# Attention in pairs of tiles, and both weight matrices converted in one pass, in a fused attention and feed-forward kernel

## The chip, the cores and the metric

The kernel runs on one core of a Trainium2 chip. TensorE (PE) multiplies, VectorE (DVE), ScalarE (ACT) and GpSimd (POOL) work on whole tiles, SyncE (SP) issues the transfers between memory and chip. The metric is the device time of one execution in microseconds, as the median of several runs.

## What is computed

For 8 batches, 8 heads, 576 positions and a head size of 64, each chunk of 64 positions attends to itself. The result, 4608 tokens of 512 values, goes through two matrices with a sigmoid gate between them:

```python
scores = scale * np.matmul(q_c, k_c.transpose(0, 1, 2, 4, 3))
scores = scores - np.max(scores, axis=-1, keepdims=True)
attn = np.exp(scores)
attn = attn / (np.sum(attn, axis=-1, keepdims=True) + 1e-09)
out = np.matmul(attn, v_c)
...
h = x @ w_in                              # 512 -> 2048
g = h * (1.0 / (1.0 + np.exp(-1.702 * h)))
return (g @ w_out).astype(np.float32)     # 2048 -> 512
```

The inputs arrive as float32, the two matrices as float64.

## The kernel before

**Tiles and blocks.** The tokens are 36 tiles of 128, in 9 blocks of 4 tiles (TB). The 2048 inner values are 16 columns (NF) of 128. One step g is one block and one column j: `h_pe` multiplies x by w_in's column into `hp`, `g_hi` and `g_lo` form the gated value, `o_pe` multiplies it by w_out's rows into the four accumulators po0 to po3, one a tile. There are 144 such steps.

**Three products for one.** x, g and both matrices are kept as a high and a low part, and each product is three matmuls over 512 columns: low by high, high by high, high by low (lines 474 to 476 for h, 509 to 511 for o; the first step works in two halves of 256 columns, lines 487 to 489).

**Weights.** The 8-byte words are turned into floats on the chip. `plan_w` does this for 32 parts, each 512 words wide, even parts for w_in and odd ones for w_out: a load, two ACT operations (`c0`, lines 173 and 174), three DVE operations (`c1`, 179, 180, 183), ACT's high part (188) and DVE's low part (191). All 32 stay on the chip and serve all 9 blocks, so conversion happens only beside the first block and a little beyond.

**Attention.** `plan_att` treats one tile of 128 tokens. Tiles 0 to 3 ("first") come before the feed-forward and keep their buffers in the slots of the last weights, four slots a tile; tiles 0 to 5 are transposed by PE (`t_pe`, line 272, `e_pe`, line 347), all others by DVE (`t_dve`, 294, `e_dve`, 367, eight transposes of 32x256). Then for each tile: scores (`s_pe`, line 317), maximum and subtraction (324, 325), the exponential on ACT (328), sum and reciprocal (332 to 335), normalisation on POOL (338), the product with v (`x_pe`, 379) and the high and low part of x (392, 395). Tiles from 4 on are worked on while the feed-forward of the block before runs. The profile lists each of the 16 float32 score matmuls of a tile, and each of the 16 with v, as two instructions, so a tile's block has 32.

**What sets the order.** Every step is handed to a `Plan` with an engine, a cost in microseconds, a rank and the buffers that it takes and gives. A greedy list scheduler runs through simulated time and lets each engine take the ready step of lowest rank; the order so found is the order in which each engine's instructions stand in the program, and nothing reorders them on the chip. SP issues all loads and stores from one queue.

Of the kernel before, what the change touches and what calls it, by code (L numbers as in the profile page):

```python
# [98 lines left out]
def tile_chunk_attention_ffn(  # L99
# [14 lines left out]
    P = 128  # L114
# [4 lines left out]
    NWP = 2 * NF  # L119
# [5 lines left out]
    NPE = 6  # L125
    NTMP = 6
    WARM = 7

# [10 lines left out]
    buffers = {b: 2 for b in ("hp", "att", "raw", "v", "tr", "e", "et", "x", "g", "ob")}  # L139
    buffers.update({f"w{p}": 1 for p in range(NWP)})  # L140
    buffers.update({f"po{t}": 1 for t in range(TB)})
    buffers.update(tmp=NTMP)
    plan = Plan(buffers)

    def att_rank(u):
        if u < TB:
            return u - 95
        return (-2, 5, 9, 10)[u - TB] if u < 2 * TB else NF * (u // TB - 1) + 4 * (u % TB) - 2
# [4 lines left out]
    def plan_w(p):  # L153
        j, part = divmod(p, 2)
        rank = 0.986 * j - (1.2 if part else 3.5)

        def words():
            word = lambda t, i: w_raw[p].bitcast(t).rearrange("p (n w) -> p n w", w=2)[:, :, i]
            return word(F32, 1), word(I32, 1), word(I32, 0), word(U32, 0)

        def load():
            w_raw[p] = raw = const.tile([P, 512], I64, tag=f"w{p}", name=f"raw_{p}")
            if part == 0:
                nc.sync.dma_start(
                    raw.rearrange("p (cc f) -> p cc f", cc=NCC),
                    w_in[:, j * P : (j + 1) * P].rearrange("(cc p) f -> p cc f", p=P),
                )
            else:
                nc.sync.dma_start(raw, w_out[j * P : (j + 1) * P, :])

        def c0():
            hf, hi, li, lu = words()
            nc.scalar.activation(hf, hf, AF.Copy, scale=2.0**-112)
            nc.scalar.activation(li, lu, AF.Copy, scale=2.0**-29)

        def c1():
            hf, hi, li, lu = words()
            w_tmp[p] = tmp = more.tile([P, 512], I32, tag="wtmp", name=f"wtmp_{p}")
# [29 lines left out]
    raw_t, v_t, t_t, e_t, s_t = {}, {}, {}, {}, {}  # L208
# [11 lines left out]
    def plan_att(u):  # L220
        first = u < TB
        pe = u < NPE
        k_act = u in (2, 5)
        rank = att_rank(u)
        slot = lambda i: f"w{NWP - 1 - (4 * u + i)}"
        res = lambda i, name: slot(i) if first else name

        def buf(i, tag, shape, name):

            pool, tag = (const, slot(i)) if first else (two, tag)  # L230
            return pool.tile(shape, F32, tag=tag, name=f"{name}_{u}")

        def load_rows():
            raw_t[u] = t = buf(0, "raw", [P, 2, H, D], "rows")
            for i, src in enumerate((q, k)):
                for b, s, o, c in spans(u * P, P):
                    nc.sync.dma_start(
                        t[o : o + c, i], src[b, :, s : s + c, :].rearrange("h s d -> s h d")
                    )

        def load_qk(i, n):

            if i == n == 0:
# [13 lines left out]

        def load_v():
            v_t[u] = t = buf(2, "v", [P, H, D], "v")
            for b, s, o, c in spans(u * P, P):  # L260
                nc.sync.dma_start(t[o : o + c], v[b, :, s : s + c, :].rearrange("h s d -> s h d"))

        def t_pe():
            raw = raw_t.pop(u)
            if first:
                ps = [ps_h.tile([P, NP, P], F32, tag="hp", name=f"qkTp_{u}_{i}") for i in range(2)]
            else:
                both = ps_a.tile([P, 2, NP, P], F32, tag="att", name=f"qkTp_{u}")
                ps = [both[:, 0], both[:, 1]]
            for i in range(2):  # L270
                for n in range(NP):
                    nc.tensor.transpose(  # L272
                        ps[i][:, n],
                        raw[:, i, 2 * n : 2 * n + 2, :].rearrange("p h d -> p (h d)"),
                        ident,
                    )
            s_t[u] = ps
            t_t[u] = buf(1, "tr", [P, 2, NP, P], "qkT")

        def t_q():  # L280
            nc.scalar.activation(t_t[u][:, 0], s_t[u][0], AF.Copy)

        def t_k():
            if k_act:
                nc.scalar.activation(t_t[u][:, 1], s_t[u][1], AF.Copy)
            else:
                nc.vector.tensor_copy(t_t[u][:, 1], s_t[u][1])

        def t_dve():
            raw = raw_t.pop(u)  # L290
            t_t[u] = t = buf(1, "tr", [P, 2, NP, P], "qkT")
            o = (u % 2) * 4
            for i in range(2):
                nc.vector.transpose(  # L294
                    t[:, i].rearrange("p n (t j) -> p n t j", j=32), raw[:, i, :, o : o + 4, :]
                )

        def s_pe():

            t = t_t.pop(u)  # L300
            e_t[u] = buf(3, "e", [P, NP, 2, CH], "e")
            if first:
                sc = ps_o.tile([P, NP, 2, CH], F32, tag=f"po{u % 2}", name=f"s_{u}")
                s_t[u] = sc
            elif pe:
                sc = ps_a.tile([P, NP, 2, CH], F32, tag="att", name=f"s_{u}")
                s_t[u] = sc
            else:
                sc = ps_a.tile([P, 2, 2, NP, CH], F32, tag="att", name=f"s_{u}")
                s_t[u] = sc[:, :, 0].rearrange("p h n j -> p n h j")  # L310
            for n in range(NP):
                for c in range(2):
                    for h in range(2):
                        r = slice(64 * h, 64 * h + 64)
                        cols = slice(64 * c, 64 * c + 64)
                        o = sc[r, n, c, :] if pe else sc[cols, h, 0, n, :]
# [12 lines left out]

        def s_sum():  # L330
            z = two.tile([P, NP, 2], F32, tag="z", name=f"z_{u}")
            nc.vector.tensor_reduce(z, e_t[u], axis=AX.X, op=ALU.add)
            nc.vector.tensor_scalar_add(z, z, 1e-9)
            s_t[u] = two.tile([P, NP, 2], F32, tag="r", name=f"r_{u}")
            nc.vector.reciprocal(s_t[u], z)  # L335

        def s_norm():
            nc.gpsimd.tensor_tensor(e_t[u], e_t[u], bc(s_t.pop(u)), op=ALU.mult)  # L338

        def e_pe():  # L340
# [267 lines left out]
```

## Time and profile before

| | before |
| --- | --- |
| median of 3 runs | 899.12 us (898.19 to 900.22) |
| profiled execution, own time | 901.2 us |
| its span | 899.4 us |
| PE busy | 875.3 us, 97% |
| DVE busy | 439.6 us, 49% |
| ACT busy | 366.4 us, 41% |
| POOL busy | 38.8 us, 4% |

A busy share is an average over the span. The first 30 us are loads and the attention of the first four tiles, until about 140 us weights are converted beside the feed-forward, and behind that the feed-forward of one block runs beside the attention of the next. What bounds a stretch is read from the row of that stretch, and from the waits of the engine that ends last in it. Times of an instruction on PE overlap with its neighbour's, so its cost is the distance from one start to the next.

### The profile page before, as it was taken

The page shows a single profiled execution, that of the slowest core. Times are in us where ns is not written, and L with a number is a line of the kernel's source. Part 1 is how long each engine was busy: PE and PEld are TensorE (multiplying, and loading weights), DVE is VectorE, ACT ScalarE, POOL GpSimd, SP SyncE. Part 2 cuts the span into 40 slices and gives each one's busy share as a digit, 9 for nine tenths or more (in the row PEclk, how much of TensorE's full clock was granted, in tenths as well). Part 3 has the DMA queues.
Part 4 walks back from the last instruction along what each step waited for, and adds up shares of the span by engine and source line. Part 5 has one row for each costly group of instructions (what it writes and reads, how often), then busy time and mean ns, then how long its engine had stood idle before and what let it go on. Part 6 is the DMA issues. An engine that isn't in the chain of part 4 may idle for free.

```text
span 899.4 us, 14557 instructions
## 1 busy us (share of the span) xinstructions
PE 875.3 (97%) x5858; PEld 705.1 (78%) x5858; DVE 439.6 (49%) x810; ACT 366.4 (41%) x554; POOL 38.8 (4%) x42
## 2 busy tenths in 40 slices
PE   7899969999999999999999999999999999999998
PEld 6688747888888888888888888888888888888886
DVE  5999996544444444444444444445444454311111
ACT  3998744333333333333433333334333333322222
POOL 1000000000000000000000000000000000000000
PEclk9799989999999999999999999999999999999999
DMA  9995232322322122212221312132210010001001
GB/s 239 319 321 140 43 57 64 63 50 51 70 66 38 29 39 63 42 31 48 64 44 26 57 59 42 31 55 65 42 30 12 24 48 1 1 1 47 1 0 48
DMA packets 199141, 55.51 MB, mean 62 GB/s; under 512 B 184225, under 2 KB 192417, under 8 KB 199073
## 3 DMA queue, kind: packets, MB, share of 16 engines
q1 hardware_dynamic: 199072, 54.57, 26.4%
q8 instruction: 46, 0.75, 0.4%
q14 instruction: 23, 0.18, 0.1%
HBM read 45.09 MB, written 9.44 MB: 61 GB/s over the span
## 4 chain that ended last, share of the span: by engine, by line
PE 95%; DVE 3%; ACT 1%; issue 0%; POOL 0%; POOLq 0%; ACTq 0%; DVEq 0%
PE po L509 15%; PE hp L474 15%; PE po L510 15%; PE hp L476 14%; PE po L511 14%; PE hp L475 14%; PE s L317 3%; PE x L379 2%; DVE eT L367 1%; PE qkTp L272 1%; DVE wtmp L180 0%; PE warm L563 0%; PE eTp L347 0%; DVE wtmp L183 0%; DVE w L191 0%
## 5 line engine op out<-in xcount | busy, mean ns | idle before, releaser
L500 DVE TENSOR_TENSOR g_l<-hp,g_h 128x512 fp32r<-128x512 f32 x144 | 99.4, 690 | 315.9 <-ACT g_h L496 314.9
L509 PE MATMUL po<-w,g_l 128*128 128x512 f32 x576 | 229.9, 399 | 0.7 <-ACT w L188 0.7
L476 PE MATMUL hp<-x_h,w 128*128 128x512 f32 x572 | 224.9, 393 | 5.7 <-DVE w L191 5.7
L474 PE MATMUL hp<-x_l,w 128*128 128x512 f32 x572 | 228.1, 399 | 1.9 <-ACT w L188 1.9
L510 PE MATMUL po<-w,g_h 128*128 128x512 f32 x576 | 227.2, 394 | 0.0
L511 PE MATMUL po<-w,g_h 128*128 128x512 f32 x576 | 225.1, 391 | 0.2 <-DVE w L191 0.2
L475 PE MATMUL hp<-x_h,w 128*128 128x512 f32 x572 | 224.4, 392 | 0.0
L495 ACT ACTIVATE hp<-hp 128x512 f32<-128x512 f32 x144 | 84.1, 584 | 172.2 <-PE hp L476 171.4
L496 ACT ACTIVATE g_h<-hp 128x512 fp32r<-128x512 f32 x144 | 86.1, 598 | 122.8 <-PE po L511 120.8
L476 PEld LDWEIGHTS hp<-x_h,w 128*128 128x128 f32 x572 | 107.8, 188 | 30.9 <-DVE w L191 7.2
L474 PEld LDWEIGHTS hp<-x_l,w 128*128 128x128 f32 x572 | 107.9, 189 | 26.9 <-ACT w L188 2.3
L509 PEld LDWEIGHTS po<-w,g_l 128*128 128x128 f32 x576 | 108.3, 188 | 26.3 <-ACT w L188 1.1
L511 PEld LDWEIGHTS po<-w,g_h 128*128 128x128 f32 x576 | 108.4, 188 | 24.5 <-DVE w L191 0.6
L475 PEld LDWEIGHTS hp<-x_h,w 128*128 128x128 f32 x572 | 108.0, 189 | 22.3
L510 PEld LDWEIGHTS po<-w,g_h 128*128 128x128 f32 x576 | 108.6, 189 | 21.2
L367 DVE STREAM_TRANSPOSE eT<-e 32x256 f32<-32x256 f32 x240 | 104.6, 436 | 36.0 <-POOL e L338 32.6
L392 ACT ACTIVATE x_h<-x 128x512 fp32r<-128x512 f32 x36 | 21.4, 595 | 129.6 <-PE x L379 129.5
L338 POOL TENSOR_TENSOR e<-e,r 128x512 f32<-128x512 f32 x36 | 38.1, 1059 | 740.9 <-DVE r L335 740.9
L328 ACT ACT_TABLE_LOAD x32 | 41.1, 1283 | 60.6 <-DVE e L325 60.6
L495 ACT ACT_TABLE_LOAD x33 | 42.3, 1283 | 0.6
L294 DVE STREAM_TRANSPOSE qkT<-raw 128x512 f32<-128x512 f32 x60 | 38.9, 685 | 1.7 <-DMA raw<-in_k_dram 1.7
L395 DVE TENSOR_TENSOR x_l<-x,x_h 128x512 fp32r<-128x512 f32 x36 | 24.8, 689 | 29.6 <-ACT x_h L392 29.6
(42 smaller groups left out, 436.0 us busy)
## 6 DMA issues: line engine op xcount, KB each, us to landing
out_dram<-ob SPq DMA_DIRECT2D x36, 256.0 KB, 2.0
v<-in_v_dram SPq DMA_DIRECT2D x32, 256.0 KB, 3.3
raw<-in_moe_w_in_dram SPq DMA_DIRECT2D x16, 512.0 KB, 7.9
raw<-in_moe_w_out_dram SPq DMA_DIRECT2D x16, 512.0 KB, 7.5
raw<-in_q_dram SPq DMA_DIRECT2D x160, 32.0 KB, 2.2
raw<-in_k_dram SPq DMA_DIRECT2D x160, 32.0 KB, 2.1
rows<-in_q_dram SPq DMA_DIRECT2D x5, 256.0 KB, 5.1
rows<-in_k_dram SPq DMA_DIRECT2D x5, 256.0 KB, 5.1
```

The source lines that it names most:

```text
L294: nc.vector.transpose(t[:, i].rearrange("p n (t j) -> p n t j", j=32), raw[:, i, :, o : o + 4, :])
L328: nc.scalar.activation(e_t[u], e_t[u], AF.Exp, scale=SCALE)
L367: nc.vector.transpose(tv[po : po + 32, :, 32 * a : 32 * a + 32], ev[pi : pi + 32, :, 32 * b : 32 * b + 32],)
L474: nc.tensor.matmul(hp, wh, xl, start=cc == 0, stop=False)
L475: nc.tensor.matmul(hp, wh, xh, start=False, stop=False)
L476: nc.tensor.matmul(hp, wl, xh, start=False, stop=cc == NCC - 1)
L495: nc.scalar.activation(h_t[g], h_t[g], AF.Gelu_apprx_sigmoid)
L496: nc.scalar.activation(gh, h_t[g], AF.Copy)
L500: nc.vector.tensor_tensor(gl, h_t.pop(g), gh.bitcast(F32), op=ALU.subtract)
L509: nc.tensor.matmul(po, gl[:, c], w[:, 0, :], start=j == 0, stop=False)
L510: nc.tensor.matmul(po, gh[:, c], w[:, 0, :], start=False, stop=False)
L511: nc.tensor.matmul(po, gh[:, c], w[:, 1, :], start=False, stop=j == NF - 1)
```

## The change

**Weights.** w_in and w_out of one column are now one weight, 1024 words wide, in one of 16 slots: two loads into its halves, then `scale` and `low` on ACT, `high` (two operations) and `join` on DVE, `part_h` on ACT and `part_l` on DVE, each over 1024. There are 3 temporary buffers instead of 6, each twice as wide.

**First tiles.** Tiles 0 to 3 use two slots each of the last eight weights, one with q, k and their transposes, freed after the scores, one with v, e and its transpose, freed after the product with v. Their q, k and v are loaded tile by tile.

**Pairs.** Tiles from 4 on are treated two at a time (`plan_pair`): one block of scores, one of products with v, and operations twice as wide between them. Pairs 4 and 6, tiles 4 to 7, are transposed by PE and normalised on DVE; later pairs are transposed by DVE, in two steps of four 32x512 transposes, and normalised on POOL. v, tr, e and et have one buffer each instead of two. The first two pairs have ranks 0 and 7.

**Plan.** Costs are adjusted, o of a block's last tile comes behind the other three, and the last two output tiles use the buffers of "raw" instead of "tr".

```diff
-    NPE = 6
-    NTMP = 6
+    NPE = 8
+    NTMP = 3
     WARM = 7
+    RANK_1 = (0.0, 7.0)
...
-    buffers = {b: 2 for b in ("hp", "att", "raw", "v", "tr", "e", "et", "x", "g", "ob")}
+    buffers = {b: 2 for b in ("hp", "att", "raw", "x", "g", "ob")}
+    buffers.update({f"w{j}": 1 for j in range(NF)})
     buffers.update({f"po{t}": 1 for t in range(TB)})
-    buffers.update(tmp=NTMP)
+    buffers.update(tmp=NTMP, v=1, tr=1, e=1, et=1)
...
+        def load(part):
             if part == 0:
+                w_raw[j] = const.tile([P, 1024], I64, tag=f"w{j}", name=f"raw_{j}")
...
+                nc.sync.dma_start(w_raw[j][:, 512:], w_out[j * P : (j + 1) * P, :])
...
+            w_tmp[j] = tmp = more.tile([P, 1024], I32, tag="wtmp", name=f"wtmp_{j}")
...
-        need = [f"{('tp', 's', 'xp', 'ep')[i]}_{u}"] if u < TB else []
-        plan.add(DMA, 1.46, rank - 5.5, load, need=need, make=f"raw_{p}", take=[f"w{p}"])
-        plan.add(ACT, 1.35, rank, c0, need=[f"raw_{p}"], make=e[0])
-        plan.add(DVE, 1.8, rank, c1, need=[e[0]], make=e[1], take=["tmp"])
-        plan.add(ACT, 0.63, rank - 3.5, c4, need=[e[1]], make=e[4])
-        plan.add(DVE, 0.7, rank - 2, c5, need=[e[4]], make=f"w_{p}", give=["tmp"])
...
+        u, kind = slot_user(j)
+        need = [f"{('s', 'xp')[kind]}_{u}"] if u < TB else []
+        e = lambda n: f"{n}_{j}"
+        plan.add(DMA, 1.6, rank - 5.5, lambda: load(0), need=need, make=e("rawi"), take=[f"w{j}"])
+        plan.add(DMA, 1.6, rank - 5.5, lambda: load(1), need=[e("rawi")], make=e("raw"))
+        plan.add(ACT, 1.1, rank, scale, need=[e("raw")], make=e("wsc"))
+        plan.add(ACT, 1.1, rank, low, need=[e("wsc")], make=e("wlow"))
+        plan.add(DVE, 1.95, rank, high, need=[e("wsc")], make=e("whigh"), take=["tmp"])
+        plan.add(DVE, 1.25, rank, join, need=[e("whigh"), e("wlow")], make=e("wj"))
+        plan.add(ACT, 1.05, rank - 3.5, part_h, need=[e("wj")], make=e("wh"))
+        plan.add(DVE, 1.25, rank - 2, part_l, need=[e("wh")], make=e("w"), give=["tmp"])
...
+            nc.vector.transpose(
+                st["tr"][:, i].rearrange("p n (t j) -> p (n t) j", j=32),
+                st["raw"][:, i].rearrange("p n t j -> p (n t) j"),
+            )
...
+            for t in range(2):
+                for n in range(NP):
+                    for c in range(2):
+                        for h in range(2):
+                            r = slice(64 * h, 64 * h + 64)
+                            cols = slice(t * P + 64 * c, t * P + 64 * c + 64)
...
+                            nc.tensor.matmul(o, tr[r, 0, n, cols], tr[r, 1, n, cols], start=True, stop=True)
...
+            eng = nc.vector if pe else nc.gpsimd
+            eng.tensor_tensor(st["e"], st["e"], bc(st["r"]), op=ALU.mult)
...
+        def e_dve(c):
...
+            for a in range(2):
+                for b in range(2):
+                    pi = 64 * c + 32 * a
+                    po = 64 * c + 32 * b
+                    nc.vector.transpose(
+                        st["et"][po : po + 32, :, 32 * a : 32 * a + 32],
+                        st["e"][pi : pi + 32, :, 32 * b : 32 * b + 32],
+                    )
...
+        rank = (RANK_1[i // 2] if b == 1 else NF * (b - 1) + 4 * i - 2)
```

**Where instructions move.** On SP's queue near the start, before: the loads of v for the first tiles, then raw_p, the words of part p (even p: w_in of column p/2, odd p: w_out).

```order
L261 DMA v_0_186<-in_v_dram 128x8x64
L261 DMA v_1_212<-in_v_dram 128x8x64
L261 DMA v_2_225<-in_v_dram 128x8x64
L261 DMA v_3_262<-in_v_dram 128x8x64
L164 DMA raw_0_295<-in_moe_w_in_dram 128x4x128
L164 DMA raw_2_321<-in_moe_w_in_dram 128x4x128
L164 DMA raw_4_329<-in_moe_w_in_dram 128x4x128
L169 DMA raw_1_359<-in_moe_w_out_dram 128x512
L164 DMA raw_6_373<-in_moe_w_in_dram 128x4x128
L169 DMA raw_3_384<-in_moe_w_out_dram 128x512
L164 DMA raw_8_391<-in_moe_w_in_dram 128x4x128
```

After, from the third first tile's v on; first_a holds q and k, first_b holds v, and raw_j has both matrices of column j:

```order
L231 DMA first_b_2_150<-in_v_dram 128x8x64
L231 DMA first_a_3_174<-in_q_dram 128x8x64
L231 DMA first_a_3_174<-in_k_dram 128x8x64
L231 DMA first_b_3_197<-in_v_dram 128x8x64
L163 DMA raw_0_206<-in_moe_w_in_dram 128x4x128
L163 DMA raw_1_245<-in_moe_w_in_dram 128x4x128
L168 DMA raw_0_206<-in_moe_w_out_dram 128x512
L163 DMA raw_2_305<-in_moe_w_in_dram 128x4x128
L168 DMA raw_1_245<-in_moe_w_out_dram 128x512
L163 DMA raw_3_326<-in_moe_w_in_dram 128x4x128
L168 DMA raw_2_305<-in_moe_w_out_dram 128x512
```

w_out of column 0 moved from the fourth place among the weights to the third, and w_in of column 2 from the third to the fourth.

On DVE at the first conversions, before (wtmp_0 and wtmp_2 are the temporaries of w_in's columns 0 and 1, z and r belong to tile 3's sum):

```order
L179 TENSOR_SCALAR wtmp_0_364<-raw_0_295 128x512
L180 SCALAR_TENSOR_TENSOR wtmp_0_364<-raw_0_295,wtmp_0_364 128x512
L183 ISA wtmp_0_364<-raw_0_295,wtmp_0_364 128x1024
L179 TENSOR_SCALAR wtmp_2_378<-raw_2_321 128x512
L180 SCALAR_TENSOR_TENSOR wtmp_2_378<-raw_2_321,wtmp_2_378 128x512
L183 ISA wtmp_2_378<-raw_2_321,wtmp_2_378 128x1024
L395 TENSOR_TENSOR x_l_0_92<-x_2_342,x_h_0_91 128x4x128
L191 TENSOR_TENSOR w_0_382<-wtmp_0_364,w_0_382 128x512
L191 TENSOR_TENSOR w_2_389<-wtmp_2_378,w_2_389 128x512
```

After (wtmp_j and w_j are column j's):

```order
L181 TENSOR_SCALAR wtmp_0_328<-raw_0_206 128x1024
L182 SCALAR_TENSOR_TENSOR wtmp_0_328<-raw_0_206,wtmp_0_328 128x1024
L302 TENSOR_REDUCE z_3_334<-first_b_3_197 128x8
L303 TENSOR_SCALAR z_3_334<-z_3_334 128x8
L305 RECIPROCAL r_3_337<-z_3_334 128x8
L188 ISA wtmp_0_328<-raw_0_206,wtmp_0_328 128x2048
L342 TENSOR_TENSOR x_l_0_92<-x_2_340,x_h_0_91 128x4x128
L181 TENSOR_SCALAR wtmp_1_372<-raw_1_245 128x1024
L182 SCALAR_TENSOR_TENSOR wtmp_1_372<-raw_1_245,wtmp_1_372 128x1024
L196 TENSOR_TENSOR w_0_369<-wtmp_0_328,w_0_369 128x1024
L188 ISA wtmp_1_372<-raw_1_245,wtmp_1_372 128x2048
L342 TENSOR_TENSOR x_l_0_92<-x_3_379,x_h_0_91 128x4x128
```

The sum of tile 3 moved from ahead of the first conversion into it, and the low part of column 1 (w_2 before, w_1 after) moved behind the first two operations of column 2.

On PE in the steady part, before: the scores of tile 16 (its 16 matmuls in one row) between o of step 44 and h of step 47.

```order
L509 MATMUL po_2_3_2646<-w_25_1445,g_l_44_3182 128x512
L510 MATMUL po_2_3_2646<-w_25_1445,g_h_44_3181 128x512
L511 MATMUL po_2_3_2646<-w_25_1445,g_h_44_3181 128x512
L317 MATMUL s_16_3252<-qkT_16_2900 64x64 x16
L474 MATMUL hp_47_3278<-x_l_2_1557,w_30_1509 128x512
L475 MATMUL hp_47_3278<-x_h_2_1556,w_30_1509 128x512
L476 MATMUL hp_47_3278<-x_h_2_1556,w_30_1509 128x512
```

After, the scores of tiles 16 and 17, in one row of 32, inside o of step 30:

```order
L642 MATMUL po_1_2_1589<-w_14_1251,g_h_30_2301 128x512
L643 MATMUL po_1_2_1589<-w_14_1251,g_h_30_2301 128x512
L443 MATMUL s_16_2411<-qkT_16_2212 64x64 x32
L641 MATMUL po_1_3_1610<-w_14_1251,g_l_30_2302 128x512
L642 MATMUL po_1_3_1610<-w_14_1251,g_h_30_2301 128x512
L643 MATMUL po_1_3_1610<-w_14_1251,g_h_30_2301 128x512
L606 MATMUL hp_33_2454<-x_l_2_1401,w_1_436 128x512
```

Two blocks of 16 became one of 32, and it stands 14 steps further ahead.

## Rows read from the trace of the kernel before

**Rows 1.** Stretches: us, PE, PEld, DVE, ACT, POOL busy (count), PE clock, DMA share, GB/s

```profile
40.00:105.00 65.00, 65.00 (x431) 52.64 (x430) 61.58 (x106) 60.85 (x105) 2.36 (x2) 1.00 0.71 199
105.00:141.00 36.00, 25.72 (x179) 18.13 (x178) 32.80 (x61) 15.85 (x22) 2.33 (x2) 0.91 0.30 52
130.00:137.00 7.00, 5.78 (x13) 4.09 (x14) 6.83 (x13) 1.26 (x2) 0.00 (x0) 0.51 0.49 82
```

**Rows 2.** Waits of PE, 100 to 145 us: us in total, times, longest

```profile
PE hp L476 <- DVE w L191: 5.7, 3, 2.8
PE hp L474 <- ACT w L188: 1.9, 1, 1.9
PE x L379 <- DVE eT L367: 1.5, 1, 1.5
```

**Rows 3.** Groups of PE, 200 to 785 us: busy us, mean ns, idle before

```profile
L509 PE MATMUL po<-w,g_l 128*128 128x512 f32 x396 | 157.9, 399 | 0.0
```

**Rows 4.** Groups of PE, 105 to 141 us, attention only

```profile
L379 PE MATMUL x<-eT,v 64*64 64x64 f32 x64 | 1.7, 224 | 1.8 <-DVE eT L367 1.5 <-PE po L511 0.2 <-issue 0.2
L317 PE MATMUL s<-qkT 64*64 64x64 f32 x32 | 0.7, 225 | 0.0
```

**Rows 5.** Order in time on PE, second column: start us, us

```profile
34.78 0.40 PE L474 MATMUL hp<-x_l,w 128*128 128x512 f32 x1
35.01 0.39 PE L475 MATMUL hp<-x_h,w 128*128 128x512 f32 x1
```

**Rows 6.** Order in time on DVE, dense conversion: start us, us

```profile
96.25 0.68 DVE L191 TENSOR_TENSOR w<-wtmp,w 128x512 fp32r<-128x512 f32 x1
96.85 0.42 DVE L179 TENSOR_SCALAR wtmp<-raw 128x512 int32<-128x512 int32 x1
...
98.64 0.70 DVE L294 STREAM_TRANSPOSE qkT<-raw 128x512 f32<-128x512 f32 x1
```

**Rows 7.** Groups of DVE, whole span, forms apart: busy us, mean ns

```profile
L367 DVE STREAM_TRANSPOSE eT<-e 32x256 f32<-32x256 f32 x240 | 104.6, 436 | 36.0 <-POOL e L338 32.6
...
L294 DVE STREAM_TRANSPOSE qkT<-raw 128x512 f32<-128x512 f32 x60 | 38.9, 685 | 1.7 <-DMA raw<-in_k_dram 1.7
```

**Rows 8.** Groups of ACT, whole span, forms apart

```profile
L173 ACT ACTIVATE raw<-raw 128x512 f32<-128x512 f32 x32 | 21.4, 668 | 0.0
```

**Rows 9.** Order in time on DVE, then on POOL, near 83 us

```profile
83.43 1.27 DVE L179 TENSOR_SCALAR wtmp<-raw 128x512 int32<-128x512 int32 x1
...
83.10 1.31 POOL L338 TENSOR_TENSOR e<-e,r 128x512 f32<-128x512 f32 x1 [33.46 <-DVE r L335]
```

**Rows 10.** Loads issued between 15.1 and 15.3 us: KB each, us to landing

```profile
raw<-in_moe_w_in_dram SPq DMA_DIRECT2D x1, 512.0 KB, 7.8
```

**Rows 11.** Order in time on PE in the steady part

```profile
228.41 0.39 PE L511 MATMUL po<-w,g_h 128*128 128x512 f32 x1
228.73 0.70 PE L317 MATMUL s<-qkT 64*64 64x64 f32 x32
229.35 0.50 PE L474 MATMUL hp<-x_l,w 128*128 128x512 f32 x1
229.69 0.39 PE L475 MATMUL hp<-x_h,w 128*128 128x512 f32 x1
...
230.85 0.39 PE L509 MATMUL po<-w,g_l 128*128 128x512 f32 x1
```

**Rows 12.** Order in time on PE, tiles transposed on PE

```profile
36.16 1.04 PE L272 MATMUL qkTp<-ident,rows 128*128 128x128 f32 x8
36.95 0.48 PE L474 MATMUL hp<-x_l,w 128*128 128x512 f32 x1
...
40.55 1.15 PE L317 MATMUL s<-qkT 64*64 64x64 f32 x32
```

**Rows 13.** Order in time on DVE in the steady part

```profile
212.26 3.60 DVE L367 STREAM_TRANSPOSE eT<-e 32x256 f32<-32x256 f32 x8 [1.22 <-POOL e L338]
...
229.53 0.69 DVE L500 TENSOR_TENSOR g_l<-hp,g_h 128x512 fp32r<-128x512 f32 x1 [4.80 <-ACT g_h L496]
```

More of the change, by code (lines that the diff above doesn't have):

```diff
@@ L425, in plan_att @@
-        plan.add(DMA, 1.46, (u - 98 if first else rank - 1.5), load_v, make=ev("v"), take=[res(2, "v")])
-        s_ps = [f"po{u % 2}"] if first else ["att", "att"]
-        plan.add(
-            PE, 1.4, rank + 0.6, s_pe, need=need, make=ev("s"),
-            take=s_ps + [res(3, "e")], give=[res(1, "tr")],
-        )
-        plan.add(DVE, 1.4, rank + 0.6, s_max, need=[ev("s")], make=ev("m"), give=s_ps)
-        plan.add(ACT, 0.55, rank + 0.6, s_exp, need=[ev("m")], make=ev("ex"), table="exp")
@@ L433, in plan_att @@
-        plan.add(DVE, 1.0, rank + 0.6, s_sum, need=[ev("ex")], make=ev("z"))
-        plan.add(POOL, 1.0, rank + 0.6, s_norm, need=[ev("z")], make=ev("n"))
-        if pe:
-            e_ps = [f"po{2 + u % 2}"] if first else ["att", "att"]
-            plan.add(
-                PE, 0.45, rank + 1.7, e_pe, need=[ev("n")], make=ev("ep"), take=e_ps, give=[res(3, "e")]
-            )
-            plan.add(ACT, 0.5, rank + 1.7, e_act, need=[ev("ep")], make=ev("et"), take=["et"], give=e_ps)
-        else:
-            plan.add(
-                DVE, 2.7, rank + 0.6, e_dve, need=[ev("n")], make=ev("et"),
-                take=["et"], give=[res(3, "e")],
+            nc.vector.tensor_tensor(x_part(x_l, u), st["x"], x_part(x_h, u).bitcast(F32), op=ALU.subtract)
@@ new lines, in plan_first @@
+        rank = u - 95
+        plan.add(DMA, 2.0, u - 103, load_qk, make=ev("rows"), take=[slot(0)])
+        plan.add(DMA, 1.0, u - 102.5, load_v, make=ev("v"), take=[slot(1)])
+        plan.add(PE, 0.95, rank, t_pe, need=[ev("rows")], make=ev("tp"), take=["hp", "hp"])
+        plan.add(ACT, 0.6, rank, t_q, need=[ev("tp")], make=ev("tq"), give=["hp"])
+        plan.add(ACT if k_act else DVE, 0.68, rank, t_k, need=[ev("tp")], make=ev("tk"), give=["hp"])
+        plan.add(
+            PE, 1.2, rank + 0.6, s_pe, need=[ev("tq"), ev("tk"), ev("v")], make=ev("s"),
+            take=[f"po{u % 2}"], give=[slot(0)],
+        )
@@ new lines, in plan_first @@
+        plan.add(DVE, 1.37, rank + 0.6, s_max, need=[ev("s")], make=ev("m"), give=[f"po{u % 2}"])
+        plan.add(ACT, 0.63, rank + 0.6, s_exp, need=[ev("m")], make=ev("ex"), table="exp")
+        plan.add(DVE, 1.1, rank + 0.6, s_sum, need=[ev("ex")], make=ev("z"))
+        plan.add(POOL, 1.07, rank + 0.6, s_norm, need=[ev("z")], make=ev("n"))
+        plan.add(PE, 0.5, rank + 1.7, e_pe, need=[ev("n")], make=ev("ep"), take=[f"po{2 + u % 2}"])
+        plan.add(ACT, 0.6, rank + 1.7, e_act, need=[ev("ep")], make=ev("et"), give=[f"po{2 + u % 2}"])
@@ new lines, in plan_pair @@
+        plan.add(DVE, 2.46, rank + 0.6, s_max, need=[ev("s")], make=ev("m"), take=["e"], give=["att", "att"])
+        plan.add(ACT, 1.05, rank + 0.6, s_exp, need=[ev("m")], make=ev("ex"), table="exp")
+        plan.add(DVE, 1.65, rank + 0.6, s_sum, need=[ev("ex")], make=ev("z"))
+        plan.add(DVE if pe else POOL, 1.23 if pe else 2.0, rank + 0.6, s_norm, need=[ev("z")], make=ev("n"))
+        if pe:
+            plan.add(PE, 0.95, rank + 1.7, e_pe, need=[ev("n")], make=ev("ep"), take=["att", "att"], give=["e"])
+            plan.add(ACT, 1.05, rank + 1.7, e_act, need=[ev("ep")], make=ev("et"), take=["et"], give=["att", "att"])
+        else:
+            for c in range(2):
+                plan.add(
+                    DVE, 2.76, rank + 0.6, lambda c=c: e_dve(c), need=[ev("n")] + ([ev("et0")] if c else []),
+                    make=ev("et" if c else "et0"), take=[] if c else ["et"], give=["e"] if c else [],
+                )
@@ L454, in tile_chunk_attention_ffn @@
+        plan.add(
+            PE, 1.4, rank + 1.5, x_pe, need=[ev("et"), ev("v1"), f"xa_{u // TB}"], make=ev("xp"),
+            take=["att", "att"], give=["et", "v"],
+        )
+        for t in range(2):
+            plan.add(ACT, 0.6, rank + 1.5, lambda t=t: x_hi(t), need=[ev("xp")], make=f"xh_{u + t}")
+            plan.add(
+                DVE, 0.69, rank + 1.5, lambda t=t: x_lo(t), need=[f"xh_{u + t}"], make=f"xl_{u + t}",
+                give=["att"],
+            )
     g_t, h_t, po_t, ob_t = {}, {}, {}, {}
@@ L458, in plan_ffn @@
         tiles = range(n * TB, n * TB + TB)
[L460 removed]
+        ob_tag = lambda t: "raw" if n == NB - 1 and t >= 2 else "ob"
         def x_alloc():
```

414 lines of the change are left out of this document (235 added, 179 removed).

## The prediction

> **What bounds the kernel now.** I read the share of TensorE (PE) by stretch first, then its waits, then who was late. From 40 to 105 us PE works without a gap, but VectorE (DVE) is busy 61.6 of 65 us beside it [rows 1]: it has no room left. From 105 to 141 us PE is busy only 25.7 of 36 us [rows 1], and the waits of that stretch are for converted weights, from DVE (L191) and ScalarE (ACT, L188) [rows 2]. Behind 145 us no wait of PE is listed; in 200 to 785 us each of its lines shows 0.0 idle, as L509 does [rows 3]. So the end is set by two things: PE's own work, and a conversion of weights that falls behind PE during the first 140 us.
>
> What that costs: of the 179 PE instructions of 105 to 141 us [rows 1], 96 are attention, three blocks of 32 [rows 4], and 83 are 512-column matmuls. Dense, one starts every 0.23 us (34.78, then 35.01) [rows 5], and a steady block of 32 takes 0.82 (below). 83 x 0.229 + 3 x 0.82 = 21.5 us, so 14.5 of the 36 us are lost: 9.1 in the three waits [rows 2], the rest in shorter ones and in the spell from 130 to 137 us, where the granted clock was 0.51 (the 1.2 GHz level) [rows 1] after PE had stood idle in pieces.
>
> **The change part by part.**
>
> *Conversion on DVE.* Today one 512-wide part takes four DVE operations, from 96.25 to 98.64 us 2.39 us in a dense run [rows 6]; a column of the feed-forward (w_in and w_out) takes two parts, 4.78. After, one pass of four operations 1024 wide does it. The trace has no 1024-wide float row; the transposes give 685 ns at 512 and 436 at 256 elements [rows 7], so 0.97 ns an element, about 0.5 us for 512 more, which I set at 0.52; L179 takes 0.42 where L191 takes 0.68 [rows 6], so +0.27 for it, half as much. The pass is then 2.39 + 0.27 + 3 x 0.52 = 4.22 us: 0.55 less per weight. If width saves nothing it is 4.78, if only the fixed part of one operation counted twice, some 0.17, were saved four times, 4.1. I take 4.22, since the fixed part in the rows is small.
>
> *Conversion on ACT.* Three operations a pass, 668 ns busy each at 512 [rows 8]. A 1024-wide one lies between 0.56 (a start-to-start interval of today) and twice that, 1.12; I take the upper end, with which ACT still runs 1 to 3 us ahead of DVE in the order of the changed kernel, so it does not enter the sum. The Trainium skill ("ScalarE: Activation LUTs", What ACT_TABLE_LOAD costs) gives 186 ns + 0.833 ns an element with immediate scale, 1039 ns at 1024 as an estimate, and the sum would be the same by it; the trace has 668 at 512, against 612 by that page.
>
> *The work between the weights.* Up to the ninth weight, DVE issues in the new order 9 passes' first two operations (1.98 each), 8 joins (1.13), 8 last parts (1.12), 7 g_l (0.61), and the pieces of tiles 4 and 5 (two copies 1.2, maximum and subtraction 2.4, sum 1.6, normalisation 1.1): 46.4 us. From 33.8 us, where the start leaves it, this ends at 80.2. PE, in its new order from 37.0 us, comes to that weight at 80.5. The same count for the weights before leaves margins of 0.2 (w2), 0.4 (w3), 1.5 (w4), 1.2, 1.3, 1.5 us, and after the ninth it opens: 3.4, 4.0, and 10 at w15. So the 14.5 us can go, since no weight is late by the rows; but the margins are thin. Rows summed this way ran 3.2 us ahead of the real DVE by 97 us in the kernel before. About half of that is collisions with GpSimd (POOL): the L179 at 83.43 took 1.27 us beside POOL's normalisation at 83.10 [rows 9], against 0.42 elsewhere, and POOL normalises twice in 40 to 105 us [rows 1]: 2 x 0.85 = 1.7. Pairs 4 and 6 now normalise on DVE, so these go, and I take a lag of 2 us at the end of the tight part: **+1.7 us** of new waits of PE (2 less the 0.3 at w8). **The 14.5 us of 105 to 141 go: -14.5.**
>
> The Trainium skill ("SBUF — State Buffer", SBUF: two separate sides) says that a DVE operation with two inputs in SBUF, or in a mode with two ports, and a GpSimd operation exclude each other for a whole instruction. The trace agrees (1.27 against 0.42). It speaks for the smaller lag; without it, lag 3.2 and a sum 1.2 higher.
>
> *The start.* The first column now needs both halves of its weight, and w_out of it stands third in the queue of loads, behind w_in of columns 0 and 1. The third load of today takes 7.8 us from its issue at 15.1, so it lands at 22.9 to 23.0 [rows 10]. From 23.0: ACT's scale 1.1 (24.1), first two DVE operations 2.0 (26.1), tile 3's sum 1.0 (27.1), join 1.1 (28.2), x_l of tile 2 0.6, the second weight's first two 2.0 (30.9), last part of weight 0 1.1 (32.0), join 1.1, x_l of tile 3 0.6, third weight's first two 2.0, last part of weight 1 at 36.9. The second column's h can start at about 37.0, today 34.78 [rows 5]: **+2.2**. A collision with POOL in this chain would add 0.85 as above; the lower end is 0, if the order on DVE runs ahead of loads that land earlier.
>
> *Pairs behind 145 us.* A block of 32 attention matmuls sits between two 512-column ones: 228.41 to 229.69 us is 1.28, less 2 x 0.23 is 0.82; the 32 themselves take 0.62 (228.73 to 229.35), so 0.20 is changeover [rows 11]. 28 tiles have two blocks each, 56 x 0.82 = 45.9 us; 14 pairs have two of 64, 28 x (0.20 + 1.24) = 40.3. PE works densely here, so all of it counts: **-5.6**. Bounds: 0 if two blocks in a row cost as before, and -11.2 if the changeover went wholly.
>
> *Pairs 4 and 6 by PE transposes.* Today only tiles 4 and 5 are transposed on PE. 8 transposes take 0.79 (36.16 to 36.95) and 0.1 around; the 32 score matmuls of this form 1.15 [rows 12], 1.28 with the changeover. Before: 2 x (0.89 + 1.28 + 0.5 + 0.82) and 4 x 0.82 for tiles 6, 7: 10.3. After: 2 x (1.78 + 2.36 + 0.9 + 1.44) = 13.0. **+2.7** on PE; in exchange DVE loses tiles 6 and 7's sixteen 32-row transposes and four 128x512 ones from its full stretch, which the 46.4 above contains.
>
> **Sum:** -14.5 + 1.7 + 2.2 - 5.6 + 2.7 = **-13.5 us**. The profiled execution took 901.2 us (span 899.4), giving 887.7; the median of the runs, 899.12, is 2.1 lower, so 885.6.
>
> Other edits cost nothing that I can see: single buffers for v, tr, e, et are covered by the 16 columns (some 90 us) that two pairs share, o of the fourth tile behind the other three is their order already, and the last output tiles use a buffer that is idle by then.
>
> **The rivals.**
>
> *The conversion still binds.* DVE gains nothing from width (0.55 x 7 weights = 3.9 us later) and the lag is the full 3.2: 6.8 us of waits at w3 to w8 instead of 1.7, and, as at 130 us, a spell at the 1.2 GHz level behind them that doubles some 6.8 us of work, 3.4. That is +3.5 to +8.5: 889 to 894. For: margins under 0.5 us at w2, w3 and w8. Against: longer operations save fixed parts in every row. 0.20.
>
> *Slower: DVE holds up g_l in the steady part.* A pair's DVE steps are twice as long, four 32x512 transposes in a piece, 2.8 us by 0.97 ns an element. g_l runs 229.53 to 230.22 [rows 13] and PE takes it at 230.85 [rows 11]: 0.6 us of slack. Had g_l to stand behind such a piece, PE would lose 2.2 us; once per pair 14 x 2.2 = 31, that is some 916. It decides against the forecast from 13.5/14, about 1.0 us a pair. Against: DVE does eight transposes, 3.60 us, in a row already (212.26) [rows 13] and PE shows no idle time there [rows 3]. 0.07.
>
> *No change.* The waits of 105 to 141 us come back at another place, as the first columns wait for loads or ACT instead: -5.6 + 2.7 + 2.2 and 0 to 2 us more, 898 to 900. Against: DVE, not ACT, is full. 0.04.
>
> *More.* The start is not later and no new wait comes: 881.7. 0.09.
>
> **How the numbers follow.** Forecast 0.60 (883 to 889), conversion binds 0.20, more 0.09, slower 0.07, no change 0.04. Predicted 885.6. The range goes from 880.5, a little under the best case, to 894, the upper end of the first rival; outside are the slower case and no change. About 0.2%, 1.8 us, is what a measurement here can tell from no change. Faster 0.89, same 0.04, slower 0.07.
>
> **What would show it.** Right: PE's waits for weights between 37 and 90 us sum to under 3 us and none stand at 105 to 141; h of the second column starts near 37.0; a weight's DVE pass takes 4.2 us; a block of 64 stands between matmuls 1.9 us apart (1.44 + 0.46); PE idle 0.0 behind 145 us. Wrong: waits over 5 us for L196 or L188 with a second spell at 1.2 GHz, idle time of L641 for g_l, or a scale or low operation of ACT late in each column.

## The result and the profile after

The changed kernel takes 889.9 us (median of four runs, 889.39 to 890.04), the kernel before 898.75 us beside it: a ratio of 0.990, interval 0.988 to 0.992. Forecast were 885.6 us, with a range of 880.5 to 894. The direction and the range held; of the 13.5 us forecast, 8.9 came. The spans of the two profiled executions, 899.4 and 888.1 us, differ by 11.3; the 2.1 us by which the profiled execution of before lay above its median had no counterpart after (profiled execution 889.83 us, median 889.9), so it must not be carried over as a constant.

Stretches of the kernel after (columns as in [rows 1]):

```profile
40.00:105.00 65.00, 64.54 (x462) 52.08 (x461) 61.72 (x69) 56.21 (x68) 0.00 (x0) 1.00 0.70 204
105.00:141.00 36.00, 36.00 (x278) 29.17 (x277) 28.85 (x36) 17.16 (x23) 1.90 (x1) 1.00 0.33 57
```

From 105 to 141 us PE is now busy 36.00 of 36 us, where it was 25.7 [rows 1], and the clock is full. The loss of that stretch is gone. What PE waits for behind its second column (us in total, times, longest) is one line, and no weight is in it:

```profile
PE qkTp L410 <- ACT eT L481: 0.3, 1, 0.3
```

The start, on PE (start us, duration us; in square brackets how long the engine stood idle and what ended it): tile 3's product with v, the first h, and the second column's h (34.78 before, [rows 5]).

```profile
30.92 1.14 PE L329 MATMUL x<-first_b 64*64 64x64 f32 x32 [0.69 <-ACT first_b L320]
31.99 0.58 PE L619 MATMUL hp<-x_l,w 128*128 128x256 f32 x1
...
36.73 0.40 PE L606 MATMUL hp<-x_l,w 128*128 128x512 f32 x1
```

Ahead of them, ACT's first conversion waits for w_out of column 0, and DVE's for ACT:

```profile
22.88 1.10 ACT L172 ACTIVATE raw<-raw 128x1024 f32<-128x1024 f32 x1 [3.72 <-DMA raw<-in_moe_w_out_dram]
...
24.01 0.69 DVE L181 TENSOR_SCALAR wtmp<-raw 128x1024 int32<-128x1024 int32 x1 [2.25 <-ACT raw L172]
```

The conversion on DVE, a stretch without gaps:

```profile
36.95 1.22 DVE L188 CUSTOM_DVE_ANT_0 wtmp<-raw,wtmp 128x2048 uint16<-128x2048 uint16 x1
38.08 0.69 DVE L181 TENSOR_SCALAR wtmp<-raw 128x1024 int32<-128x1024 int32 x1
38.81 1.23 DVE L182 SCALAR_TENSOR_TENSOR wtmp<-raw,wtmp 128x1024 int32<-128x1024 int32 x1
39.95 0.68 DVE L632 TENSOR_TENSOR g_l<-hp,g_h 128x512 fp32r<-128x512 f32 x1
40.55 1.22 DVE L196 TENSOR_TENSOR w<-wtmp,w 128x1024 fp32r<-128x1024 f32 x1
41.68 1.22 DVE L188 CUSTOM_DVE_ANT_0 wtmp<-raw,wtmp 128x2048 uint16<-128x2048 uint16 x1
```

Start to start, join 1.13, L181 0.73, L182 1.14, g_l 0.60, L196 1.13: a column's pass is 4.13 us where two passes of 2.39 were needed [rows 6].

A pair's scores in the steady part of PE:

```profile
171.51 0.39 PE L643 MATMUL po<-w,g_h 128*128 128x512 f32 x1
171.83 1.16 PE L443 MATMUL s<-qkT 64*64 64x64 f32 x64
172.92 0.50 PE L641 MATMUL po<-w,g_l 128*128 128x512 f32 x1
173.26 0.39 PE L642 MATMUL po<-w,g_h 128*128 128x512 f32 x1
```

Between the o ahead of the block and the second matmul behind it lie 1.75 us; less two matmuls of 0.23 that is 1.29 for 64, against 0.82 for 32 [rows 11].

So every stage did what was forecast or more, and still 2.2 us of the span are missing. They are in a place that the forecast took for fixed. In 800 to 850 us there is no attention and no conversion in either kernel, only the feed-forward, and PE is busy all the time. Before, then after:

```profile
800.00:850.00 50.00, 50.00 (x221) 41.22 (x220) 7.55 (x11) 12.30 (x21) 0.00 (x0) 1.00 0.06 21
```

```profile
800.00:850.00 50.00, 50.00 (x218) 40.62 (x217) 7.12 (x11) 11.12 (x19) 0.00 (x0) 1.00 0.06 22
```

The same 50 us hold three PE instructions fewer. Four matmuls of this stretch in the kernel after:

```profile
803.53 0.40 PE L641 MATMUL po<-w,g_l 128*128 128x512 f32 x1
803.77 0.40 PE L642 MATMUL po<-w,g_h 128*128 128x512 f32 x1
804.01 0.39 PE L643 MATMUL po<-w,g_h 128*128 128x512 f32 x1
804.24 0.39 PE L641 MATMUL po<-w,g_l 128*128 128x512 f32 x1
```

They start 0.24, 0.24 and 0.23 us apart. Averaged over the start-to-start distances of neighbouring 512-column matmuls behind 150 us (those over 300 ns left out; 2943 pairs before, 2971 after), it was 229.1 ns and is 231.6. This distance is called the cadence below. The program has 3444 such matmuls (143 steps of 24, and 12 of the first step), so by an estimate that is 8.6 us. With each distance given to the earlier matmul of its pair, it is mostly o's (229.5 to 233.6 ns), less h's (228.7 to 229.6).

### The profile page after: what moved, and what is told of

The parts are those of the page before. It is cut to its first block, busy times and chain, and to the rows that moved or that the text cites. A ratio compares the mean times of both kernels' runs of the same rounds, so it can differ in the third digit from the quotient of the medians.

```text
span 888.1 us, 14202 instructions
## 1 busy us (share of the span) xinstructions
PE 870.6 (98%) x5882; PEld 705.6 (79%) x5882; DVE 389.8 (44%) x511; ACT 317.6 (36%) x459; POOL 32.4 (4%) x24
## 4 chain that ended last, share of the span: by engine, by line
PE 94%; SPq 2%; DMA 2%; ACT 1%; issue 0%; DVE 0%; ACTq 0%
PE po L641 16%; PE po L642 15%; PE po L643 15%; PE hp L608 15%; PE hp L607 15%; PE hp L606 15%; PE s L443 2%; PE x L503 2%; SPq L231 1%; DMA raw<-in_moe_w_in_dram 1%; DMA rows<-in_k_dram 1%; ACT raw L172 0%; PE qkTp L410 0%; SPq L168 0%; SPq L163 0%
## 5 line engine op out<-in xcount | busy, mean ns | idle before, releaser
L606 PE MATMUL hp<-x_l,w 128*128 128x512 f32 x572 | 223.9, 391 | 0.0
L490 DVE STREAM_TRANSPOSE eT<-e 32x512 f32<-32x512 f32 x112 | 78.7, 702 | 21.0 <-PE x L503 17.2
L470 POOL TENSOR_TENSOR e<-e,r 128x1024 f32<-128x1024 f32 x14 | 26.7, 1906 | 611.4 <-DVE r L466 325.5
L425 DVE STREAM_TRANSPOSE qkT<-raw 128x1024 f32<-128x1024 f32 x28 | 34.7, 1241 | 13.8 <-PE s L443 11.3
L515 ACT ACTIVATE x_h<-x 128x512 fp32r<-128x512 f32 x32 | 17.5, 595 | 33.2 <-PE x L503 33.1
L463 DVE TENSOR_REDUCE z<-e 128x16 f32<-128x1024 f32 x16 | 19.5, 1218 | 9.5 <-ACT e L459 8.8
L443 PEld LDWEIGHTS s<-qkT 64*64 64x64 f32 x1024 | 18.2, 135 | 5.8 <-issue 5.8
```

Source lines behind the costliest of these rows:

```text
L425: nc.vector.transpose(st["tr"][:, i].rearrange("p n (t j) -> p (n t) j", j=32), st["raw"][:, i].rearrange("p n t j -> p (n t) j"),)
L443: nc.tensor.matmul(o, tr[r, 0, n, cols], tr[r, 1, n, cols], start=True, stop=True)
L490: nc.vector.transpose(st["et"][po : po + 32, :, 32 * a : 32 * a + 32], st["e"][pi : pi + 32, :, 32 * b : 32 * b + 32],)
L606: nc.tensor.matmul(hp, wh, xl, start=cc == 0, stop=False)
```

## Experiments

**Theory A:** the cadence of PE depends on where its operands lie in SBUF, the memory on the chip from which it reads them. The change moved everything: slots of 8 KB, and behind them x and the gated value g. In the built programs the start addresses modulo 512 bytes are, before: weights 128, x 128, g 320; after: weights 128, x 128, g 0. **Rival B:** it is the order on PE, or the new layout of h and l parts within a slot.

First, the layout within a slot alone (`x_layout`), matrix first, then part:

```diff
-            wt[j] = const.tile([P, 2, 1024], F32R, tag=f"w{j}", name=f"w_{j}")
-            nc.scalar.activation(wt[j][:, 0, :], w_tmp[j].bitcast(F32), AF.Copy)
+            wt[j] = const.tile([P, 2, 2, 512], F32R, tag=f"w{j}", name=f"w_{j}")
+            two_m = w_tmp[j].bitcast(F32).rearrange("p (m f) -> p m f", m=2)
+            nc.scalar.activation(wt[j][:, :, 0, :], two_m, AF.Copy)
...
-            w = wt[j][:, :, 512:]
+            w = wt[j][:, 1]
```

> The changed kernel, with each slot ordered by matrix first (w_in high, w_in low, w_out high, w_out low) instead of by part first; the operations and their order are the same, only the addresses differ. After the change a 512-column matmul starts 231.6 ns behind the one ahead of it, before it was 229.1. Theory A (the addresses of the new slots cost PE 2 to 4 ns a matmul): the interval moves, towards 229, and with some 3400 matmuls the time falls by up to 8 us, to 882. Rival B (the cadence comes from the order on PE or from the instructions' own position): interval 231.6 as it is, time 889 to 890.5.

Measured: 889.94 us, 231.6 ns a matmul. A shift by 2 KB within the slot changes nothing; the layout within a slot is not the cause.

Then g, by unused bytes ahead of its two buffers; n is 40 floats (320 bytes for the two) in `x_gpad`, 8 in `x_g64`, 16 in `x_g128`. The kernel before got the same line, with 24 in `b_gpad` and 40 in `b_g128`. The instructions and their order stay. In the built programs the buffers that stand behind g move with it: those of the output and of the conversion, and in the kernel before some of the attention's too. In 800 to 850 us, where of all these only the output's are in use, for a few copies, the cadence differs as it does over the whole run, so g itself is enough.

```diff
         def g_hi():
+            if g == 0:
+                two.tile([P, n], F32, tag="pad", name="pad")
             gh = two.tile([P, BT], F32R, tag="gh", name=f"g_h_{g}")
```

> The changed kernel, with 320 unused bytes a partition ahead of the buffers of the gated value g, so that g lies 192 bytes modulo 512 from the weights, as in the kernel before, instead of 384. Nothing else moves. Theory A (addresses): if the distance of g to the weights is what counts, o's matmuls go from 233.7 back to some 229.5 ns and the time to 882 to 884; h's matmuls stay. Rival B: no change, 889 to 890.5.

Measured: 879.62 us, ratio to before 0.979 (0.977 to 0.980). 10.3 us, by moving unchanged buffers, and more than the 6 to 8 us expected. The cadence of o's matmuls fell as expected, to 229.4 ns; but h's, which were expected to stay, fell too, from 229.6 to 227.4, though h reads x and the weights alone.

> The kernel before, with 192 unused bytes a partition ahead of g's buffers, so that g lies 384 bytes modulo 512 from the weights, as in the changed kernel. Theory A (distance of g to the weights): o's matmuls slow from 229.4 to some 233 ns, time +5 to +7 us, 904 to 906. Rival B: 898 to 900.

Measured: 907.1 us, ratio 1.009 (1.008 to 1.011). The old kernel, with g where the new one has it, loses 8.5 us, a little more than expected. Rival B has fallen: the order on PE is untouched in both.

> The changed kernel with g's buffers moved up by 64 bytes a partition (g at 64 modulo 256, the weights at 128, x at 128). What has been seen: g at 0 modulo 256 gives a matmul every 231.6 ns, g at 64 gives 228.4 to 229.1. Theory A1 (only the last 256 bytes of the address count): 228.4 ns and 879 to 880 us, as with 320. Rival A2 (modulo 512, where 320 is good and 64 was not seen): anything up to 890.

Measured: 879.5 us, as with 320. 64 and 320 are alike modulo 256, so places are given modulo 256 below; this pair is the only one that was compared for it.

> The changed kernel with g's buffers moved up by 128 bytes a partition, so that g lies as the weights and x do modulo 512 (128). Theory A1a (what counts is g's own address; 0 modulo 128 is bad): 231.6 ns and 889 to 890 us. Theory A1b (what counts is the distance to the weights; equal is bad or good): o's matmuls as those of h, where x and the weights lie alike, some 228 to 229 ns, 879 to 882 us.

Measured: 874.76 us (874.36 to 876.24), ratio 0.973 (0.972 to 0.975), below what either theory expected. Equal places are good, not bad. Four matmuls of the same kind as above start 0.22 to 0.23 us apart:

```profile
803.28 0.39 PE L643 MATMUL po<-w,g_l 128*128 128x512 f32 x1
803.50 0.39 PE L644 MATMUL po<-w,g_h 128*128 128x512 f32 x1
803.73 0.39 PE L645 MATMUL po<-w,g_h 128*128 128x512 f32 x1
803.96 0.39 PE L643 MATMUL po<-w,g_l 128*128 128x512 f32 x1
```

and the 50 us hold 223 instructions:

```profile
800.00:850.00 50.00, 50.00 (x223) 41.39 (x222) 6.24 (x9) 10.63 (x18) 0.00 (x0) 1.00 0.00 0
```

> The changed kernel with x's buffers and g's both moved up by 320 bytes, so that x too leaves the weights' 128 modulo 512 and g lies at 320. If distance or address counts for h as for o, h's matmuls leave 227.4 ns (g at 320 alone): down by 1 to 3 ns and 874 to 878 us, or up by as much and 882 to 885 us; if x's place does not count, 879 to 880.

```diff
         def x_alloc():
+            if n == 0:
+                two.tile([P, 40], F32, tag="pad", name="pad")
             x_h[n] = two.tile([P, NCC, BT], F32R, tag="xh", name=f"x_h_{n}")
```

Measured: 886.76 us; h's matmuls slow to 231.2 ns from 227.4 with g alone at this place, a little more than expected. So x counts too, and taking x away from the weights costs 7 us:

```profile
800.00:850.00 50.00, 50.00 (x219) 40.69 (x218) 6.81 (x10) 11.32 (x20) 0.00 (x0) 1.00 0.03 11
```

Is it the address or the distance? In `x_g128` weights, x and g all lie at 128. `x_all0` moves all three up to 0, where g alone was slowest:

```diff
+    const.tile([P, 96], F32, tag="pad0", name="pad0")
     ident = const.tile([P, P], F32, tag="ident", name="ident")
...
+                two.tile([P, 16], F32, tag="pad", name="pad")
```

> The changed kernel with weights, x and g all moved up so that all three lie at 0 modulo 512 instead of 128. Theory of distance: 226.9 ns a matmul, 874 to 876 us, as with all at 128. Theory of the operand's own address (0 is bad, 128 is good): 231 ns or more, 889 us or more.

Measured: 874.11 us (873.11 to 874.78), 226.9 ns. What counts is where the three lie to one another, not the address of each.

> The kernel before, with g's buffers moved up by 320 bytes a partition, to the same place modulo 512 as the weights and x (128). Theory (a matmul is fastest where its moving and stationary operands lie alike): 226.9 ns a matmul instead of 229.1, 3456 x 2.2 = 7.6 us less, 891 to 892. Rival (the gain seen in the changed kernel belongs to its own slots): 898 to 900.

Measured: 893.41 us, ratio 0.993 (0.992 to 0.995), 227.1 ns. A little less than expected (6.1 for 7.6 us), and the waits for weights stand there unchanged:

```profile
PE hp L476 <- DVE w L191: 5.5, 3, 2.8
PE hp L474 <- ACT w L188: 1.9, 1, 1.9
PE x L379 <- DVE eT L367: 1.5, 1, 1.5
```

The table, in ns from start to start, means of h's and of o's matmuls behind 150 us (worked out from the starts in each trace, each distance given to the earlier matmul; "x to weights" is x's place less the weights'):

| kernel | x to weights, mod 256 | g to weights, mod 256 | h | o | us |
| --- | --- | --- | --- | --- | --- |
| before | 0 | 192 | 228.7 | 229.5 | 898.8 |
| b_gpad | 0 | 128 | 229.4 | 233.4 | 907.1 |
| b_g128 | 0 | 0 | 227.3 | 226.9 | 893.4 |
| after | 0 | 128 | 229.6 | 233.6 | 889.9 |
| x_gpad, x_g64 | 0 | 192 | 227.4 | 229.4 | 879.6, 879.5 |
| x_g128, x_all0 | 0 | 0 | 226.8 | 227.0 | 874.8, 874.1 |
| x_xg320 | 64 | 192 | 231.2 | 230.0 | 886.8 |

The table also shows what the theory of distance does not explain. In the kernel after, in `x_gpad` and in `x_g128`, x lies at the weights' place, yet h's matmuls take 229.6, 227.4 and 226.8 ns: the place of g acts on matmuls that do not read g. A rival is that ACT and DVE, which write g while h runs, hold PE up. Taking only those of h's matmuls beside which neither ACT, DVE nor POOL has an instruction running, it is still 231.5 ns in the kernel after against 226.7 in `x_g128`, and 228.4 in `b_gpad` against 226.7 in `b_g128`. So the writes are not the whole reason; how an o matmul's operands slow the h matmuls near it is not shown. The distance between a matmul's own two operands alone does not set its cadence.

**The waits of 105 to 141 us: what removed them?** `b_npe8` gives the kernel before one part of the change, tiles 6 and 7 transposed by PE.

```diff
-    NPE = 6
+    NPE = 8
```

> The kernel before, with tiles 6 and 7 transposed by PE too; weights in 32 parts, one tile at a time, normalisation on POOL as before. Theory (DVE's full stretch is what makes weights late, and the transposes of tiles 6 and 7 are 2 x (3.6 + 1.25) = 9.7 us of it against 1.2 us of copies): the waits for weights behind 100 us, 9.1 us, fall to 0 to 2, PE takes 2 to 3 us more for the transposes: 888 to 893. Rival (width of the conversion is needed): waits stay over 5 us, 897 to 902.

Measured: 892.07 us, ratio 0.992 (0.990 to 0.993). What PE waits for behind 31 us (us in total, times, longest), and the stretch where it lost 14.5 us:

```profile
PE s L317 <- DVE x_l L395: 3.0, 1, 3.0
```

```profile
105.00:141.00 36.00, 32.96 (x310) 25.91 (x309) 32.77 (x60) 21.04 (x30) 3.37 (x3) 0.91 0.39 82
```

No weight is waited for any more. One wait of 3.0 us has come in its place, for x of an earlier tile. In the kernel before, relieving DVE of the transposes of two tiles is by itself enough for the weights.

`a_half` takes the width back on DVE, in the changed kernel: its four operations of the conversion (L181, L182, L188 and L196) are each issued as two of 512. The edit of one of them:

```diff
-            nc.vector.tensor_tensor(w_tmp[j], w_tmp[j], li, op=ALU.add)
+            for a in (slice(0, 512), slice(512, 1024)):
+                nc.vector.tensor_tensor(w_tmp[j][:, a], w_tmp[j][:, a], li[:, a], op=ALU.add)
```

> The changed kernel with every DVE operation of the conversion issued as two of 512 instead of one of 1024; ACT's stay 1024 wide, the order stays. Theory (width saves 0.55 us a weight on DVE, and the margins to PE at the third to ninth weight are 0.2 to 1.4 us): the ninth weight comes 8 x 0.55 = 4.4 us later and PE waits some 4 to 5 us in 37 to 90 us, with or without a half-clock spell behind it: 893 to 899. Rival (margins are wide, the gain was in the order and in the pairs): under 1 us of waits, 889.5 to 891.

Measured: 891.81 us, 1.9 more than the changed kernel, between the two. DVE:

```profile
45.66 0.42 DVE L182 TENSOR_SCALAR wtmp<-raw 128x512 int32<-128x512 int32 x1
...
47.78 1.29 DVE L200 TENSOR_TENSOR w<-wtmp,w 128x512 fp32r<-128x512 f32 x2
48.99 0.69 DVE L424 COPY qkT<-qkTp 128x512 f32<-128x512 f32 x1
49.59 1.28 DVE L190 CUSTOM_DVE_ANT_0 wtmp<-raw,wtmp 128x1024 uint16<-128x1024 uint16 x2
50.79 0.69 DVE L636 TENSOR_TENSOR g_l<-hp,g_h 128x512 fp32r<-128x512 f32 x1
```

2.12 + 1.21 + 1.20 = 4.53 us a pass (the first two operations from 45.66 to 47.78, the low part to 48.99, the join from 49.59 to 50.79), 0.40 more than 4.13, not 0.55. From 40 to 105 us DVE has no room (64.08 of 65 us), and PE waits 1.1 us for g_l, which stands in the same queue; behind 105 us nothing comes back:

```profile
40.00:105.00 65.00, 63.83 (x456) 50.87 (x456) 64.08 (x109) 55.48 (x66) 0.00 (x0) 1.00 0.68 201
105.00:141.00 36.00, 35.98 (x278) 28.93 (x277) 29.80 (x46) 18.06 (x23) 1.91 (x1) 1.00 0.34 59
```

```profile
PE po L645 <- DVE g_l L636: 1.1, 1, 1.1
```

Width is worth 1.9 us here. It is not what emptied 105 to 141 us.

**The start.** `a_swap` exchanges the loads of w_in of column 1 and w_out of column 0, all engines' orders as they are; `swapped` issues the other one's transfer.

```diff
+            if (j, part) in ((0, 1), (1, 0)):
+                return swapped(part)
```

> The changed kernel, with two loads exchanged: w_out of column 0 comes second among the weights, w_in of column 1 third. All orders on the engines stay. Theory (the start hangs on the landing of column 0's second half, at 22.8 us): it lands at 21.5, everything behind it comes 1.3 us earlier, the second column's h starts at 35.4 instead of 36.7, time 888.6. Rival (the start hangs on the attention of tile 3 and on DVE): under 0.3 us.

Measured: 888.93 us (888.64 to 889.04), 1.0 less. First h and second column's h:

```profile
30.98 0.58 PE L631 MATMUL hp<-x_l,w 128*128 128x256 f32 x1
...
35.66 0.39 PE L618 MATMUL hp<-x_l,w 128*128 128x512 f32 x1
```

Both come 1.0 to 1.1 us earlier (31.99 and 36.73 in the kernel after). ACT's first conversion starts 1.7 us earlier (22.88 in the kernel after):

```profile
21.15 1.14 ACT L184 ACTIVATE raw<-raw 128x1024 f32<-128x1024 f32 x1 [0.64 <-DMA raw<-in_moe_w_out_dram]
```

The start does hang on that load, though not all of its gain arrives at PE.

> The changed kernel with g at the weights' place modulo 512 and the two loads exchanged. If the two gains add (15.1 and 1.0 us on 889.9): 873.5 to 874.

Measured: 873.68 us (873.64 to 874.02), ratio 0.972 (0.970 to 0.973): below both kernels by 25.8 and 16.2 us, and the lowest median of all, though `x_all0`, at 874.11, is no further off than its own runs are from one another.

## Why the prediction was right, and where it was not

- *The stretch from 105 to 141 us (-14.5).* Right, by [rows 1] against the first fence above. The reason given, a DVE that is full, is right too; `b_npe8` shows that taking the transposes of tiles 6 and 7 off DVE would have been enough. The busy share by itself does not tell: from 40 to 105 us DVE is as busy as before (61.72 us, 61.58 [rows 1]) and no weight is late. It finishes the join of 11 columns there, where it was 20 half-wide ones; and in 105 to 141 us the sixteen transposes of tiles 6 and 7, 7.0 us, are gone.
- *New waits (+1.7).* 0.5 us (65.00 less 64.54 in 40 to 105 us). The lag of DVE against the sum of rows was 0.8 us at the ninth weight (81.0 us for 80.2), not 2. The price of a pass, 4.22 us, was 4.13. The rival "the conversion still binds" fell with it; `a_half` comes nearest to it, and costs 1.9, not 3.5 to 8.5.
- *Conversion on ACT.* The 668 ns hold for two of the three operations, the third (L188) took 625; 1024 wide they take 1.15, 1.15 and 1.06 us. The sum has no term from it, and no wait for a weight from ACT is listed.
- *The collisions of DVE and POOL* went with the normalisation of pairs 4 and 6, and POOL has no work in 40 to 105 us (0.00 in the first fence above). The Trainium skill ("SBUF — State Buffer", SBUF: two separate sides) calls the port that the two share an exclusive lock. The smaller lag fits that; how much of it is due to that was not separated.
- *The start (+2.2).* 1.95 us (36.73 less 34.78). The chain named, load of w_out, then ACT, then DVE, stands in the trace: ACT's first conversion starts at 22.88 us, where the landing was put at 22.9 to 23.0. `a_swap` shows that the start moves with that load.
- *Pairs in the steady part (-5.6).* Mis-sized: a block of 64 takes 1.29 us and not 1.44, so 28 x 1.29 = 36.1 against 56 x 0.827 = 46.3, -10.2 (0.827 is the mean of the blocks behind 150 us). I had put the 0.15 us between the last small matmul and the next large one to the 32 matmuls; it is changeover. Of 0.82 us 0.35 is changeover, not 0.20.
- *Pairs 4 and 6 by PE (+2.7).* +2.0 to +2.4 by the starts in the two traces (10.2 us before, 12.2 to 12.6 after, by whether the gaps that only some blocks have are counted), for the same reason.
- *What was not in the sum:* the matmul's own cadence, +8.6 us. I counted every 512-column matmul at 0.229 us in both kernels, and wrote that the other edits cost nothing that I could see. The change moved buffers, and that was enough. With it the sum is -14.5 + 0.5 + 2.0 - 10.2 + 2.0 + 8.6 = -11.6 us, for 11.3 in the spans.

The runs also give the two parts without this sum. With g at the same distance from the weights, the two kernels differ by 17.2 us (`b_gpad` and the kernel after), 18.6 (`b_g128` and `x_g128`) and 19.1 (the kernel before and `x_gpad`): that is what the change saves apart from the place of g, where 13.5 were forecast. The place of g costs 8.5 us in the kernel before (`b_gpad`) and 10.3 in the one after (`x_gpad`). The sum of the other terms, -20.2, is 1 to 3 us larger than these differences; it was read from an execution of the kernel before that lay 2.1 us above its median.

That g_l is held up in the steady part, the slower rival, did not happen: no wait for it is listed behind 36.7 us. The point forecast was as near as it was because the terms that came out better (4.6 us for the pairs, 1.2 for the waits, some 0.9 for start and transposes) covered 6.7 of the 8.6 us that were not in the sum. That is luck: errors of opposite sign, above all a block of 64 priced too high and a cadence taken as fixed, cancelled in large part. With g where the kernel before has it the changed kernel takes 879.6 us (`x_gpad`), which lies below the range.

What stays open is why the places count, and why those of o's operands count for h: the trace shows when a matmul starts, not what it waited for.

## What to carry to other kernels

Where PE is the bound, take its cadence from start to start in a stretch without other work, for each kind of matmul, and compare it across versions before looking at anything else: 2.5 ns in 229 were worth 8.5 to 10.3 us, as much as the whole measured change. When a change moves buffers, try their places with unused bytes ahead of them; here all three operand buffers at the same place modulo 256 bytes were the fastest of the places tried, in both kernels. And measure every kind of matmul, not only the kind that reads the moved buffer: h got slower with the place of g. And a changeover is measured with both its gaps, from the last matmul ahead to the second one behind.

## What the runs showed of the hardware

A float32r matmul of 512 columns with its weight load started every 226.9 ns in the kernel after where x, g and the weights all lay at equal addresses modulo 256 (all at 128 modulo 512, or all at 0), and every 227.1 in the kernel before. With g 128 bytes from the weights it was 233.6 ns for o's matmuls and 229.6 for h's, which do not read g; with g 192 bytes away 229.4 and 227.4; with x 64 bytes from the weights as well, 231.2 for h's. Both kinds of operand count, and a shift by 2048 bytes within a slot did not. On the kernel after, the best place against the worst tried is worth 15 us in 890, with the same instructions in the same order.

A block of small 64x64 matmuls between two 512-column ones cost 0.35 us of changeover and about 15 ns for each small instruction (0.82 us for 32, 1.29 for 64).
